# A fused attention and feed-forward kernel: the last quarter of the second weight matrix is issued by another engine's queue

## The chip, the cores and the metric

One core of a Trainium2 chip. The metric is the device time of one execution in microseconds, median of three runs: 299.79 us (299.73 to 300.87). The engines are TensorE (PE, matmuls), VectorE (DVE), ScalarE (ACT), GpSimd (POOL) and SyncE (SP, which here only issues DMA transfers). SyncE and GpSimd each issue DMA transfers into a queue of their own; the transfers of all queues are carried by the core's 16 DMA engines.

## The reference

Windowed attention over 8 batches of 8 heads, 576 positions of 64, window 32 to each side; its output, as 4608 tokens of 512, goes through a feed-forward layer with a tanh GELU.

```python
scores = scale * np.matmul(q, k.transpose(0, 1, 3, 2))
mask = np.abs(pos[:, None] - pos[None, :]) <= 32
scores = np.where(mask, scores, -1e9)
attn = exp(scores - max); attn /= attn.sum(-1) + 1e-9
x = matmul(attn, v).transpose(0, 2, 1, 3).reshape(4608, 512)
h = x @ w_in                                   # (512, 2048)
g = 0.5 * h * (1 + tanh(c * (h + 0.044715 * h**3)))
out = g @ w_out                                # (2048, 512)
```

## The kernel before

The tokens are worked on in nine tiles (`t`) of 512. For each tile there is a first product (`ffn_in`, L545: `ph` or `mm` from `xT` and `w_in16`), a GELU on ScalarE (L553, into `gT`), and a second product with `w_out16`. While tile t's second product runs, the attention of batch t + 1 is worked in between its matmuls, so that tile t + 1 finds its `xT`. Every engine runs its instructions in the order in which the program writes them; nothing is reordered (`manual_schedule`). An instruction that waits holds up all that stands behind it on its engine, and a transfer is issued when its engine comes to it.

The weights arrive as float32 and are cast to float16. `w_out` (2048 x 512) comes in four quarters of 1 MB, `wo[0]` to `wo[3]`, each into a staging tile `wst` of 128 x 4 x 512 from a pool of five buffers (`stage_w`). A quarter has four blocks of 128 rows (`c` = 0 to 3); `load_w_out(i, w, c0, c1)` (L236) issues the transfer of blocks c0 to c1 of quarter i, and `cast_w` (L240 to L242) casts blocks on VectorE, ScalarE or GpSimd. The batch's values `vr` come in four transfers of 256 KB (`vs(0)` to `vs(3)`, L158) and a tail (`vs(4)`, L156); the tails of queries and keys come by `tails()` (L166, L168).

All of these are issued by SyncE. The program writes, after the first weights are cast (L844 and after), the issues in this order: quarter 1, queries and keys, quarter 2's lower half, more queries and keys, `vs(0)`, quarter 2's upper half, `vs(1)`, quarter 3's lower half, `vs(2)`, `vs(3)`, quarter 3's upper half, `vs(4)`, the tails. After them come the loads of batch 2 (L195, L188, L202, L203), whose place in the program is later, but whose buffers are free early.

Tile 0's second product is `ffn_out_0(t4, fc)` (L691): 64 matmuls of 128 x 512, one for each step i = 0 to 63 of the loop at L951, in the order `ORDER_0`: i = 0 to 15 use w_out's blocks 0 to 3 (quarter 0), 16 to 31 blocks 4 to 7, 32 to 47 blocks 8 to 11, and 48 to 63 blocks 12 to 15 (quarter 3), with blocks 12 and 13 first and 14 and 15 from i = 56 on. What is worked in at which step is written in `PLAN_0`, a table from i to actions:

```python
PLAN_0 = {...  16: "m0", 19: "k2", ..., 38: "w5", 39: "m-1", 41: "r3@1", 43: "e1",
          47: "s3@0 v-1@1 d0 w3 e2", 48: "m3 d1", 52: "e3 d2 d3 x-1", 53: "n2@0",
          55: "u3", 57: "p0@0 p2@1 x0 x1", ...}
```

- `k2` (i = 19): casts of queries and keys of head pair 2 on VectorE, and of batch 0's query tails on GpSimd (L334).
- `e0` (35), `e1`, `e2`, `e3`: the cast of one value block on GpSimd (L329). `d0` to `d3`: copies of value halves on VectorE (L222, L224).
- `w2`, `w5` (28, 38): casts of quarter 2's lower and upper half; in `w5` GpSimd casts block 10 and ScalarE block 11.
- `w3` (47): casts of quarter 3's lower half, block 12 on VectorE, 13 on GpSimd. `u3` (55): the upper half, block 14 on GpSimd, 15 on ScalarE; it also places batch 2's loads (`load_qk(2)`).
- `s`, `m`, `n`, `p`, `v`, `x`: scores and exponentials, masks, sums, products with the values, and the products that give `xT`.

Of the kernel before, what the change touches and what calls it, by code (L numbers as in the profile page):

```python
# [78 lines left out]
def kernel(  # L79
# [9 lines left out]
    nc = tc.nc  # L89
# [115 lines left out]
    def load_v(b, cs=range(4)):  # L205
        V = Vs[b % 2]
        for c in cs:
            nc.gpsimd.dma_start(V[:, c, :, :],  # L208
                                v[b, :, 128 * c:128 * c + 128, :].rearrange("h p d -> p h d"))
# [17 lines left out]
    w_out_v = moe_w_out.rearrange("(c p) f -> p c f", p=128)  # L227

    def stage_w():
        return stage.tile([128, 4, 512], FP32, name="wst", tag="stage")  # L230
# [2 lines left out]
        nc.sync.dma_start(w[:, c0:c1, :], w_in_v[:, c0:c1, 512 * i:512 * i + 512])  # L233
        return w

    def load_w_out(i, w, c0=0, c1=4):  # L236
        nc.sync.dma_start(w[:, c0:c1, :], w_out_v[:, 4 * i + c0:4 * i + c1, :])
        return w

    def cast_w(w, dst, on_dve=(0, 1), cs=range(4), on_act=()):  # L240
# [581 lines left out]
    qk, tails, vs = load_early(1)  # L822
    qk(0)
    wo = [load_w_out(0, stage_w())]
    qk(2)

# [21 lines left out]
    cast_w(wi[1], w_in16[:, :, 512:1024], (0, 2))  # L848
    cast_w(wi[2], w_in16[:, :, 1024:1536], (0, 2))
    wo.append(load_w_out(1, stage_w()))  # L850
    qk(4)
    tails_0("q")
    wo.append(load_w_out(2, stage_w(), 0, 2))
    qk(6)
    vs(0)
    load_w_out(2, wo[2], 2, 4)
    vs(1)
    wo.append(load_w_out(3, stage_w(), 0, 2))
    vs(2, 3)
    load_w_out(3, wo[3], 2, 4)  # L860
    vs(4)
    tails()

# [30 lines left out]
    for t in range(NT):  # L894
# [56 lines left out]
        for i in range(113 if t else 65):  # L951
            if t > 1 and i == 4 and b + 1 < B:
                nc.gpsimd.tensor_copy(after, KLs[b % 2][:, 3, 0:1])  # L953
                load_v(b + 1)
            if t == 1 and i == 94:
                for c in range(4):
                    nc.gpsimd.tensor_copy(Vs[1][:, c, :, :], vrs[3][:, c, :, :])
# [116 lines left out]
```

## Time and profile before

| | |
|---|---|
| median of three runs | 299.79 us (299.73 to 300.87) |
| the profiled execution: its time, its span | 298.71 us, 297.0 us |
| mean granted TensorE clock | 0.999 |
| busy: PE, DVE, ACT, POOL | 287.1, 209.2, 196.4, 89.4 us |
| SyncE's queue (q1) | 38.67 MB, 61.6 % of 16 engines' span |
| GpSimd's queue (q0) | 10.83 MB, 23.0 % |
| first GpSimd transfer in the profile | 76.42 us |
| tile 0's second product (L691) | 34 to 56 us |

The span is the time from the first to the last instruction; the time of the execution is a little longer. The profile is of one execution. All times inside it are microseconds from the span's start. "A <- B" means that A's engine sat idle until B ended. In lists of transfers the last number is the time from the issue to the landing.

### The profile page before, as it was taken

How to read it: one execution, taken by the hardware profiler on the slowest of the kernel's cores; microseconds unless marked ns; L12 is line 12 of the kernel's file. 1: busy time of each engine (PE TensorE's matmuls, PEld its weight loads, DVE VectorE, ACT ScalarE, POOL GpSimd, SP SyncE). 2: the span in 40 equal slices, each digit the busy share in tenths (PEclk: the TensorE clock that was granted, in tenths of full speed). 3: DMA queues.
4: the chain of work that ended last, by engine and by line, in shares of the span. 5: the costliest groups of instructions: out<-in, count | busy, mean ns of one | idle time of the engine just before them, and what ended most of it. 6: DMA issues, size and time to landing. Idle time of an engine off the chain costs nothing.

```text
span 297.0 us, 7282 instructions
## 1 busy us (share of the span) xinstructions
PE 287.1 (97%) x2949; PEld 184.7 (62%) x2949; DVE 209.2 (70%) x466; ACT 196.4 (66%) x315; POOL 89.4 (30%) x141
## 2 busy tenths in 40 slices
PE   7889999999999999999999999999999999999993
PEld 3534444446874587458844884488547867786783
DVE  4662475997986676868686879576966776964772
ACT  4876756778587876678657965695669557705800
POOL 3435415201407731406080606060800050015000
PEclk9999999999999999999999999999999999999999
DMA  7999999989999998989997997999594040004013
GB/s 216 263 297 383 366 280 263 264 178 202 291 192 191 235 233 156 145 167 244 150 193 116 253 145 158 142 227 170 102 175 38 0 116 29 2 13 131 0 35 109
DMA packets 116615, 51.01 MB, mean 172 GB/s; under 512 B 98391, under 2 KB 110167, under 8 KB 116582
## 3 DMA queue, kind: packets, MB, share of 16 engines
q1 hardware_dynamic: 91684, 38.67, 61.6%
q0 software_dynamic: 23776, 10.83, 23.0%
q10 hardware_dynamic: 1122, 1.06, 1.1%
q8 instruction: 23, 0.38, 0.6%
q14 instruction: 10, 0.08, 0.1%
HBM read 36.70 MB, written 9.44 MB: 155 GB/s over the span
## 4 chain that ended last, share of the span: by engine, by line
PE 80%; DMA 13%; DVE 2%; SPq 2%; ACT 1%; issue 1%; POOL 0%
PE mm L719 32%; PE mm L545 17%; PE ph L545 15%; DMA wst<-in_moe_w_out_dram 7%; DMA wst<-in_moe_w_in_dram 5%; PE pu L597 3%; PE ps_s L436 3%; PE ps_d L463 2%; DMA tr<-in_k_dram 2%; PE ps_o L473 2%; SPq L254 2%; PE mm L597 1%; PE ps_od L473 1%; PE ps_od L463 1%; PE mm L691 1%; PE py L719 1%
## 5 line engine op out<-in xcount | busy, mean ns | idle before, releaser
L545 PEld LDWEIGHTS <-w_in 128*128 128x128 f16 x512 | 49.7, 98 | 56.9 <-POOL w_in L835 0.5
L545 PE MATMUL ph<-xT,w_in 128*128 128x512 f16 x256 | 64.1, 379 | 0.4 <-POOL w_in L835 0.4
L545 PE MATMUL mm<-xT,w_in 128*128 128x512 f16 x256 | 64.1, 379 | 0.0
L681 POOL DMA_DIRECT2D out_dram<-y x55 | 32.3, 597 | 83.8 <-DVE y L748 75.5
L553 ACT ACTIVATE gT<-mm 128x512 f16<-128x512 f32 x60 | 35.6, 598 | 33.1 <-PE mm L545 32.5
L719 PEld LDWEIGHTS <-s 128*128 128x128 f16 x512 | 49.3, 98 | 7.1 <-DVE s L662 0.6
L719 PE MATMUL mm<-t,s 128*128 128x256 f16 x376 | 45.2, 273 | 0.3 <-DVE y L732 0.2
L662 DVE TENSOR_TENSOR s<-gT 128x512 f16<-128x512 f16 x64 | 27.2, 426 | 19.0 <-ACT gT L553 18.8
L719 PEld LDWEIGHTS <-gT 128*128 128x128 f16 x384 | 36.2, 98 | 6.5
L553 ACT ACTIVATE gT<-ph 128x512 f16<-128x512 f32 x58 | 32.2, 600 | 10.9 <-PE ph L545 10.9
L449 ACT ACTIVATE pe<-ps_s 128x960 f16<-128x960 f32 (+1 forms) x31 | 29.5, 974 | 13.9 <-PE ps_s L436 13.8
L719 PE MATMUL mm<-w_out,gT 128*128 128x256 f16 x256 | 32.6, 273 | 0.0
L104 ACT ACT_TABLE_LOAD x18 | 23.1, 1283 | 2.2 <-issue 1.9
L498 ACT ACTIVATE lt<-ps_d 128x480 f32<-128x480 f32 (+2 forms) x28 | 15.6, 556 | 10.4 <-PE ps_d L463 6.9
L499 ACT ACTIVATE lt<-lt 128x480 f32<-128x480 f32 (+3 forms) x36 | 21.1, 585 | 1.1
L458 DVE TENSOR_TENSOR pe<-pe,band 128x960 f16<-128x960 f16 x28 | 18.6, 683 | 2.3 <-ACT pe L449 2.3
L473 PEld LDWEIGHTS <-V 128*64 128x64 f16 x520 | 13.8, 111 | 6.3 <-DVE V L218 1.2
L719 PE MATMUL mm<-t,gT 128*128 128x256 f16 x128 | 16.1, 273 | 0.0
L208 POOL DMA_DIRECT2D V<-in_v_dram x16 | 14.3, 909 | 1.1 <-POOL after L953 0.4
L662 DVE TENSOR_TENSOR s<-s,gT 128x512 f16<-128x512 f16 x32 | 13.9, 434 | 1.1
L719 PE MATMUL mm<-w_out,s 128*128 128x256 f16 x120 | 14.6, 273 | 0.0
L508 DVE TENSOR_TENSOR xT<-ps_o,lt 128x480 f16<-128x480 f32 (+5 forms) x26 | 13.4, 536 | 1.1 <-PE ps_o L473 1.1
(146 smaller groups left out, 387.1 us busy)
## 6 DMA issues: line engine op xcount, KB each, us to landing
kr<-in_k_dram SPq DMA_DIRECT2D x31, 256.0 KB, 10.0
qr<-in_q_dram SPq DMA_DIRECT2D x6, 1024.0 KB, 6.9
wst<-in_moe_w_in_dram SPq DMA_DIRECT2D x7, 512.0 KB, 8.4
wst<-in_moe_w_out_dram SPq DMA_DIRECT2D x2, 1024.0 KB, 11.6
wst<-in_moe_w_out_dram SPq DMA_DIRECT2D x4, 512.0 KB, 5.8
qr<-in_v_dram SPq DMA_DIRECT2D x8, 256.0 KB, 5.6
V<-in_v_dram POOLq DMA_DIRECT2D x16, 128.0 KB, 8.8
qr<-in_q_dram SPq DMA_DIRECT2D x7, 256.0 KB, 6.9
```

The source lines that it names most:

```text
L104: nc.scalar.add_instruction(mybir.InstLoadActFuncSet(name=nc.get_next_instruction_name(), act_func_set_id=which, ins=[], outs=[]))
L208: nc.gpsimd.dma_start(V[:, c, :, :], v[b, :, 128 * c:128 * c + 128, :].rearrange("h p d -> p h d"))
L449: nc.scalar.activation(pe, ps[:, :, 0:w], AF.Exp, scale=SCALE)
L458: nc.vector.tensor_tensor(pe, pe, m.rearrange("k (o j) p -> k o j p", o=1).broadcast_to(list(pe.shape)), op=ALU.mult)
L473: nc.tensor.matmul(o[64 * h:64 * h + 64, cols].rearrange("d (j p) -> d j p", j=4)[:, :, p0 - q0:p1 - q0], Vs[b % 2][:, slot, 2 * pr + h, : ...
L498: nc.scalar.activation(lt[:, 0:n], d[:, 0:n], AF.Ln)
L499: nc.scalar.activation(lt[:, 0:n], lt[:, 0:n], AF.Exp, scale=-1.0)
L545: nc.tensor.matmul(ph, w_in16[:, dc, fc * 128:fc * 128 + 128], xT[:, dc, t * 512 % RING:t * 512 % RING + 512], start=(dc == 0), stop=(dc = ...
L553: nc.scalar.activation(gTs[t][:, fc, :], phs[fc], AF.Gelu_apprx_tanh)
L662: nc.vector.tensor_tensor(dst, x, y, op=op)
L681: eng.dma_start(out_v[b, j, q0 + p:q0 + p + e, cols], yo[m:m + e, cols])
L719: nc.tensor.matmul(pys["apart"][:, 0:256] if apart else py[:, blk, :], lhsT, wino[w][:, f, :], start=(new and i % (8 if one else 16) == 0) ...
```

## The change

`load_w_out` gets a parameter for the queue. The two issues of quarter 3 are taken out of SyncE's order (`vs(1)`, `vs(2)`, `vs(3)`, `vs(4)` then follow one another), while the staging buffer is taken at the same place. They are written into step i = 20 of tile 0's loop, on GpSimd's queue, both halves one after the other. On GpSimd they stand directly behind the cast of query tails (L334, i = 19) and ahead of the first value cast (L329, i = 35). The casts of the quarter stay where they are (i = 47 and 55), and wait for GpSimd's transfers instead of SyncE's.

```diff
-    def load_w_out(i, w, c0=0, c1=4):
-        nc.sync.dma_start(w[:, c0:c1, :], w_out_v[:, 4 * i + c0:4 * i + c1, :])
+    def load_w_out(i, w, c0=0, c1=4, queue=nc.sync):
+        queue.dma_start(w[:, c0:c1, :], w_out_v[:, 4 * i + c0:4 * i + c1, :])
         return w
...
     vs(1)
-    wo.append(load_w_out(3, stage_w(), 0, 2))
+    wo.append(stage_w())
     vs(2, 3)
-    load_w_out(3, wo[3], 2, 4)
     vs(4)
     tails()
...
                 load_v(b + 1)
+            if t == 0 and i == 20:
+                load_w_out(3, wo[3], 0, 2, nc.gpsimd)
+                load_w_out(3, wo[3], 2, 4, nc.gpsimd)
             if t == 1 and i == 94:
```

## The prediction

> **What bounds the kernel now.** I read the page's busy shares first (PE 287.1 us of a span of 297.0: 97 %), then TensorE's own waits, then the chain of waits in order of time, then SyncE's and GpSimd's timelines around tile 0's second product, last the DMA answers. The chain of waits, in order of time (start, duration, what):
>
> ```profile
> 26.55 11.24 DMA wst<-in_moe_w_out_dram
> 37.81 8.40 DMA wst<-in_moe_w_out_dram
> 46.26 0.62 POOL w_out L242
> 46.92 0.38 PE mm L691
> ...
> 49.04 0.36 PE ps_s L436 x16
> 49.43 0.98 ACT pe L449
> 50.43 0.66 DVE pe L458
> ...
> 53.28 0.30 DVE V L224
> 53.62 0.98 PE ps_od L473 x40
> ```
>
> Until 46.9 us the end is set by a transfer: the upper half of w_out's third quarter, issued at 37.81, lands 8.40 us later, GpSimd casts its first block, TensorE goes on. From there on the chain runs over TensorE's order, an exponential, a mask and copies of values, and after 56 us almost only over TensorE. So whoever delays that landing delays everything; and nothing here can make it earlier, since it is issued before the place of the change. TensorE's waits between 34 and 57 us (us in total, times, longest):
>
> ```profile
> PE mm L691 <- POOL w_out L242: 0.9, 2, 0.5
> PE mm L691 <- DVE w_out L242: 0.6, 1, 0.6
> ```
>
> The 0.6 is at 33.96 us, ahead of the change. The 0.9 is 0.48 us at 46.92 (the landing above) and 0.40 us at 52.85 (a cast of the last quarter's upper half). Only the 0.40 belongs to the transfers that the change moves. SyncE issues (start, duration):
>
> ```profile
> 37.81 2.18 SPq L237 DMA_DIRECT2D wst<-in_moe_w_out_dram  x1
> 40.04 1.06 SPq L158 DMA_DIRECT2D vr<-in_v_dram  x1
> 41.20 2.28 SPq L237 DMA_DIRECT2D wst<-in_moe_w_out_dram  x1
> 43.53 2.64 SPq L158 DMA_DIRECT2D vr<-in_v_dram  x2
> 46.21 2.42 SPq L237 DMA_DIRECT2D wst<-in_moe_w_out_dram  x1
> ```
>
> and GpSimd works:
>
> ```profile
> 40.94 0.60 POOL L334 CAST t<-tr 64x512 f16<-64x512 f32 x1 [2.47 <-DMA tr<-in_q_dram]
> 44.58 0.82 POOL L329 CAST V<-vr 128x512 f16<-128x512 f32 x1 [3.04 <-DMA vr<-in_v_dram]
> 46.26 0.61 POOL L242 CAST w_out<-wst 128x512 f16<-128x512 f32 x1 [0.86 <-DMA wst<-in_moe_w_out_dram]
> 47.38 0.61 POOL L329 CAST V<-vr 128x512 f16<-128x512 f32 x1 [0.51 <-DMA vr<-in_v_dram]
> 48.97 0.63 POOL L242 CAST w_out<-wst 128x512 f16<-128x512 f32 x1 [0.98 <-DMA wst<-in_moe_w_out_dram]
> 49.66 1.90 POOL L329 CAST V<-vr 128x512 f16<-128x512 f32 x2
> 52.05 0.75 POOL L242 CAST w_out<-wst 128x512 f16<-128x512 f32 x1 [0.49 <-DMA wst<-in_moe_w_out_dram]
> ```
>
> GpSimd waits for almost every transfer: first values at 44.6, third quarter at 46.2, second values at 47.4, the moved halves at about 48.9 and 52.0. One queue delivers these in the order of issue, about as fast as they are used. The stretches show DMA busy at 0.95 to 1.24 from 36 to 48 us; the six of one microsecond from 42 to 48 moved 305, 309, 268, 347, 302 and 250 GB/s, a mean of 297.
>
> **The change, part by part.** *Removed from SyncE:* two issues, 2.28 + 2.42 = 4.70 us. Behind them stand the third and fourth values, batch 1's tails, and batch 2's queries and keys; they are issued up to 2.3 and 4.7 us earlier. The values end at GpSimd's casts, which the last of them meets without a wait even now (49.66, two in a row); the later loads feed tile 1, where TensorE shows no wait for a transfer. Worth nothing, then; at best the 0.40 us at 52.85, and not even that by the chain, which passes that moment over the mask and the copies of values, not over the weight cast. A gain is thus bounded by 0.40 us.
>
> *Added to GpSimd:* two issues of 512 KB. In the changed program they stand after the cast of query tails (L334, ends 40.94 + 0.60 = 41.54) and before the first cast of values (44.58). The staging buffer is free (its earlier contents were last read at 30.2), so they wait for nothing. Nearest rows: 611 ns for a store of 128 rows on this queue, 909 ns for a value load of 1,024 pieces; so 1.2 to 1.8 us for two, I take 1.2 (these have 256 pieces each). Both bounds fit in the 3.04 us of waiting before 44.58, so what is queued behind them (the value cast and the weight casts) loses nothing; without that cover it would be 1.2 to 1.8 us on the values. GpSimd's later transfers take other semaphores, which costs nothing, as their waits reach eight transfers back as before.
>
> *Moved:* 1 MB, from a place behind the third quarter and between the values to a second queue that is open beside SyncE's. The first half's issue stays where it was (41.55 against 41.20), the second comes 4 us early. This is the part that can cost. How early does its data flow? The shortest landings on GpSimd's queue are 3.4 us for a 160 KB store and 3.6 us for a 64 KB load at 83.2; so the first bytes count from 41.55 + 3.4 = 44.95. At that time SyncE's queue still owes 46.21 - 44.95 = 1.26 us of the third quarter. If both queues share evenly, these 1.26 us take 2.52: the landing slides by 1.26 us. Bounds: 0, if the older queue loses nothing; and 1,048,576 B / 297 GB/s = 3.53 us, if the whole moved megabyte goes first. That queues do take from each other this kernel shows, with the same sequence (one 1 MB query load, four key loads) twice, at 51 and at 73 us, and with a crowd from 105 us on (size, us to landing):
>
> ```profile
> kr<-in_k_dram SPq DMA_DIRECT2D x4, 256.0 KB, 5.4
> kr<-in_k_dram SPq DMA_DIRECT2D x4, 256.0 KB, 7.2
> out_dram<-yo POOLq DMA_DIRECT2D x2, 256.0 KB, 6.5
> kr<-in_k_dram SPq DMA_DIRECT2D x2, 256.0 KB, 13.0
> ```
>
> Alone 5.4 us; beside two 256 KB stores of GpSimd's (76.4 us) 7.2; beside stores and value loads 13.0. Half a megabyte beside it cost 1.8 us, which lies on the side of an even share. I take 1.26.
>
> The Trainium skill has a rule against this change: "DMA: Bandwidth & Descriptors", section "Queues, rings and completion order", says that each DMA engine goes round the queues that have work, a packet at a time, so a second queue gives no new engines and takes its turns from the first. By that rule the third quarter's landing slides by about the 1.26 us; by the reading that a second queue is free it would slide by 0. The 5.4 against 7.2 us agrees with the rule.
>
> *What is late next.* The values go behind the third quarter on SyncE's queue. Work from 44.95 on: 1.26 us for the third quarter, 3.53 for the moved quarter, three values of 262,144 B / 297 GB/s = 0.88, so 2.65; 7.44 in all, and the last value lands by 52.39. GpSimd casts it in 0.80 (mean 803 ns), then the last quarter's third block in 0.73 (mean 726 ns): 53.92, TensorE 0.05 later at 53.97, against 52.85 now: 1.12 us. That lies inside the 1.26 by which TensorE is late already, so the two don't add; the copies of values on VectorE (52.97 + 1.26 = 54.23) find the last cast done at 53.19. The moved halves themselves, at half of 297 GB/s, land at 44.95 + 3.53 = 48.5 and 52.0, against 48.9 and 52.0 now: in time for a TensorE that runs 1.26 us late.
>
> **Sum.** -0 (SyncE's slots) + 0 (GpSimd's issues, hidden) + 1.26 (third quarter) + 0 (values, inside it) = +1.26 us. Nothing downstream takes it back: TensorE is busy nearly without a gap after 56 us. The profiled execution took 298.71 us (span 297.0); with the sum 299.97. The median of the runs is 1.08 us above that execution, so 299.79 + 1.26 = 301.05, which I give as 301.1: 0.42 % slower. A measurement of this kernel can tell from no change what lies over 0.5 %, 1.5 us, so this is just inside "no change".
>
> **Rivals.**
>
> *The queues don't collide in time.* GpSimd's transfers take longer to start than 3.4 us, or the older queue keeps its pace. For it: in the crowd from 97 us on, stores of 112 to 144 KB on GpSimd's queue needed 9.1 to 9.7 us, so the newcomer can be the one that loses. Then the third quarter lands at 46.21 as now, and at best the 0.40 us at 52.85 goes: 299.4 to 299.8. Against it: DMA is full in that stretch, and 5.4 became 7.2. This rival is not slower.
>
> *The moved quarter goes first, or is itself late.* Slower, by one mechanism: GpSimd's queue gets more than its half while the third quarter is under way, so that the cast at 46.26 and the matmul behind it wait for up to the whole megabyte: 3.53 us, 303.3. It decides from a landing 1.5 us late on. For it: 2 KB rows against the 256 B rows of the values, and a DMA that was full before. Against it: the same 9.1 to 9.7 us stores. In the middle between even and whole, (1.26 + 3.53) / 2 = 2.4 us: 302.2.
>
> *It does not do what it says.* If the cast at L334 waited longer for its tails (now it ends 2.47 us of waiting at 40.94), the two issues would go out later. For it: they stand behind that wait on GpSimd. Against it: the tails are issued at 30.12, ahead of all that moves. At 43.5 instead of 41.55 the first bytes count from 46.9, after the third quarter: the first half, alone, would land 1.77 us (524,288 B / 297 GB/s) later, at 48.7, so 299.8.
>
> **How the numbers follow.** Even sharing 0.46 (0.6 to 2.0 us late: 300.4 to 301.8, a little more than half of it below the bound of 301.3); no collision 0.20, with the late issue 0.24; the moved quarter first 0.25; a gain beyond all that I see 0.05. Faster by over 0.5 % needs 1.5 us, where I find 0.40: 0.05. Within 0.5 %: 0.24 and 0.26 of the sharing case, 0.50. Slower by over 0.5 %: 0.25 and the other 0.20 of sharing, 0.45. The range takes in the no-collision case with a few tenths of scatter and the whole megabyte: 299.2 to 303.2; the likeliest case's own range is 300.4 to 301.8.
>
> **What would show it.** In the changed profile: GpSimd's two issues directly after 41.5, 0.6 to 0.9 us each; the weight cast now at 46.26 at about 47.5, and the matmul at 46.92 at about 48.2; the score matmuls of 49.04 at about 50.3; no wait of TensorE for the last quarter beyond 0.4 us; SyncE's values and batch 2's queries issued 2 to 5 us earlier. If the cast still comes at 46.3, the sharing is wrong; if it comes after 48, GpSimd's queue took more than half. If TensorE waits for the casts of the moved quarter (L242 at i = 48 or 56) by more than now, the new queue is the slow one, and my sum has the wrong term.

## The result and the profile after

The changed kernel takes 300.48 us (median of 21 runs, 298.86 to 303.12); the kernel before, in as many runs, 299.35 us (298.38 to 300.95). The ratio is 1.0031, 95 % interval 1.0017 to 1.0046: slower by 0.93 us (0.5 to 1.4); the medians alone lie 1.13 us apart. The profiled execution of the changed kernel has a span of 298.9 us, against 297.0.

The chain of waits of the changed kernel, in order of time (start, us, what):

```profile
25.80 11.11 DMA wst<-in_moe_w_out_dram
...
36.92 2.12 SPq L237
...
42.86 9.04 DMA vr<-in_v_dram
...
51.96 0.64 POOL V L329
52.59 0.57 POOL w_out L242
...
53.21 0.38 PE mm L691
```

Before, this stretch hung on the landing of the third quarter (its upper half, blocks 10 and 11) at 46.2. Now it hangs on the last value: landed 9.04 us after its issue, cast by GpSimd, and only then GpSimd's next instruction, the cast of w_out's block 14, for which TensorE waits. TensorE's own waits over the whole run:

```profile
PE mm L691 <- POOL w_out L242: 2.0, 2, 1.1
PE ps_s L436 <- DMA KT<-k: 1.5, 1, 1.5
```

The first were 0.9 us before. They are the waits at i = 40 and i = 56; first the kernel before, then the changed one:

```profile
46.92 0.38 PE L691 MATMUL mm<-w_out,gT 128*128 128x512 f16 x1 [0.48 <-POOL w_out L242]
52.85 0.38 PE L691 MATMUL mm<-w_out,gT 128*128 128x512 f16 x1 [0.40 <-POOL w_out L242]
```

```profile
46.40 0.38 PE L691 MATMUL mm<-w_out,gT 128*128 128x512 f16 x1 [0.81 <-POOL w_out L242]
53.21 0.38 PE L691 MATMUL mm<-w_out,gT 128*128 128x512 f16 x1 [1.14 <-POOL w_out L242]
```

The wait for transposed keys (`KT`) is at 225 us and is treated below: it comes and goes in both kernels. SyncE and then GpSimd of the changed kernel in order of time (start, us, what, and in brackets the idle time before):

```profile
36.92 2.12 SPq L237 DMA_DIRECT2D wst<-in_moe_w_out_dram  x1
39.09 6.37 SPq L158 DMA_DIRECT2D vr<-in_v_dram  x3
45.50 3.54 SPq L156 DMA_DIRECT2D vt<-in_v_dram  x1
49.15 0.72 SPq L166 DMA_DIRECT2D tr<-in_q_dram  x1
```

```profile
40.92 1.65 POOL L237 DMA_DIRECT2D wst<-in_moe_w_out_dram  x2
43.93 0.61 POOL L329 CAST V<-vr 128x512 f16<-128x512 f32 x1 [1.35 <-DMA vr<-in_v_dram]
45.73 0.61 POOL L242 CAST w_out<-wst 128x512 f16<-128x512 f32 x1 [1.19 <-DMA wst<-in_moe_w_out_dram]
46.87 0.61 POOL L329 CAST V<-vr 128x512 f16<-128x512 f32 x1 [0.52 <-DMA vr<-in_v_dram]
48.27 0.61 POOL L242 CAST w_out<-wst 128x512 f16<-128x512 f32 x1 [0.79 <-DMA wst<-in_moe_w_out_dram]
50.68 0.68 POOL L329 CAST V<-vr 128x512 f16<-128x512 f32 x1 [1.79 <-DMA vr<-in_v_dram]
51.96 0.64 POOL L329 CAST V<-vr 128x512 f16<-128x512 f32 x1 [0.60 <-DMA vr<-in_v_dram]
52.54 0.61 POOL L242 CAST w_out<-wst 128x512 f16<-128x512 f32 x1
```

This execution ran 0.8 us ahead of the other one until 34 us, so times are to be compared from the second product's start: its first matmul is at 33.17, against 33.96. SyncE got rid of two issues (4.70 us), yet the query tails go out at 49.15, against 49.38, no earlier by that start: the three values now take 6.37 us to issue (1.06 + 2.64 before) and the value tail 3.54 (0.61). What was freed went into the next issues, which took longer. On GpSimd the last cast, of block 14, no longer waits for its own transfer: it starts at 52.54, when the cast ahead of it ends. The moved transfers' landings (size, us from issue), the two halves:

```profile
wst<-in_moe_w_out_dram POOLq DMA_DIRECT2D x1, 512.0 KB, 7.3
wst<-in_moe_w_out_dram POOLq DMA_DIRECT2D x1, 512.0 KB, 8.0
```

So the upper half, issued at about 41.8, was there at about 49.8, 2.7 us before GpSimd came to its cast; the value that is cast ahead of it came at 51.9.

VectorE waits for the same value. Its last copies of values, which the products with the values need:

```profile
52.63 0.67 DVE L222 COPY V<-V 64x512 f16<-64x512 f16 x1 [0.51 <-POOL V L329]
53.31 0.28 DVE L224 COPY V<-V 64x512 f16<-64x512 f16 x1
```

They end at 53.59, 2.50 us before tile 1's first matmul (56.09). In the kernel before, where these products wait for the last copy, it ends 2.49 us before that matmul (53.57, 56.06). So in the changed kernel the late value reaches TensorE by two paths that end together: over block 14's cast, which the chain names, and over the copies.

As a yardstick I take the length of tile 0's second product, from the start of its first matmul (L691) to that of tile 1's first (L545), in each profile. Times and ratios are of many runs, the lengths of one execution each.

| kernel | second product, us | ratio to before (95 %) |
|---|---|---|
| before; again | 22.10; 22.16 | 1 |
| the change; again; a third time | 22.92; 24.47; 22.35 | 1.0031 (1.0017 to 1.0046) |
| e1, upper half on GpSimd | 23.01 | 1.0057 (1.0034 to 1.0080) |
| e2, lower half on GpSimd | 21.90 | 1.0013 (0.9997 to 1.0029) |
| e3, both halves early, on SyncE | 22.76 | 1.0022 (0.9999 to 1.0044) |
| e4, both on GpSimd, at i = 35 | 24.55 | 1.0057 (1.0034 to 1.0080) |
| e5, lower at i = 20, upper at i = 38 | 22.72 | 0.9999 (0.9984 to 1.0015) |
| e6, the change, block 14 cast first | 22.53 | 1.0009 (0.9992 to 1.0027) |
| e7, no transfer of the quarter | 22.08 | one execution only |
| c1, before, third quarter ahead of values | 22.05 | 1.0016 (0.9996 to 1.0037) |
| c2, the change, likewise | 22.35 | 1.0025 (1.0001 to 1.0049) |

### The profile page after: what moved, and what is told of

It is laid out like the page before. It is cut to its first block, busy times and chain, and to the rows that moved or that the text cites. A ratio compares the mean times of both kernels' runs of the same rounds, so it can differ in the third digit from the quotient of the medians.

```text
span 298.9 us, 7280 instructions
## 1 busy us (share of the span) xinstructions
PE 286.3 (96%) x2949; PEld 184.0 (62%) x2949; DVE 210.6 (70%) x466; ACT 196.4 (66%) x315; POOL 89.7 (30%) x143
## 3 DMA queue, kind: packets, MB, share of 16 engines
q10 hardware_dynamic: 1122, 1.06, 1.1%
## 4 chain that ended last, share of the span: by engine, by line
PE 76%; DMA 16%; SPq 4%; DVE 1%; ACT 1%; issue 0%; POOL 0%
PE mm L719 32%; PE mm L545 16%; PE ph L545 14%; DMA wst<-in_moe_w_in_dram 5%; DMA wst<-in_moe_w_out_dram 4%; PE pu L597 3%; DMA vr<-in_v_dram 3%; PE ps_s L436 3%; DMA KT<-k 3%; PE ps_d L463 2%; PE ps_o L473 2%; DMA tr<-in_k_dram 2%; SPq L254 2%; SPq L158 1%; PE mm L597 1%; PE ps_od L473 1%
## 5 line engine op out<-in xcount | busy, mean ns | idle before, releaser
L545 PEld LDWEIGHTS <-w_in 128*128 128x128 f16 x512 | 49.6, 98 | 56.9 <-issue 0.5
L545 PE MATMUL ph<-xT,w_in 128*128 128x512 f16 x256 | 64.1, 379 | 0.4 <-POOL w_in L835 0.4
L545 PE MATMUL mm<-xT,w_in 128*128 128x512 f16 x256 | 64.1, 379 | 0.0
L436 PE MATMUL ps_s<-QT,KT 64*64 64x128 f16 (+3 forms) x576 | 13.5, 216 | 1.8 <-DMA KT<-k 1.5
L436 PEld LDWEIGHTS <-KT 64*64 64x64 f16 x576 | 10.0, 106 | 7.7 <-issue 3.8
```

Source lines behind the costliest of these rows:

```text
L436: nc.tensor.matmul(sides[h][64 * half:64 * half + 64, 4 * n * r:4 * n * r + 4 * n].rearrange("k (j p) -> k j p", j=4)[:, :, p0 - q0:p1 - q ...
L545: nc.tensor.matmul(ph, w_in16[:, dc, fc * 128:fc * 128 + 128], xT[:, dc, t * 512 % RING:t * 512 % RING + 512], start=(dc == 0), stop=(dc = ...
```

## The experiments

The theory, formed on the profile above: the upper half is needed last but arrives early, at the cost of values that are needed before it. The rivals: the second queue costs as such; the third quarter's landing is all of the cost; the cost lies in later tiles.

**Half of the change at a time: e1 and e2.**

```diff
-    wo.append(stage_w())
+    wo.append(load_w_out(3, stage_w(), 0, 2))      # e1: lower half on SyncE
...
-                load_w_out(3, wo[3], 0, 2, nc.gpsimd)
                 load_w_out(3, wo[3], 2, 4, nc.gpsimd)
```

> Only the upper half of the last quarter goes by GpSimd's queue at i = 20; the lower half stays on SyncE between the second and third values. Theory (the values, 256 B rows behind a shared DMA, come late, and GpSimd's cast of block 14 stands behind the last value's cast): half the megabyte beside the values, so the last value lands about half as late as with the whole (1.4 us late there, so about 0.7), TensorE's wait at i = 56 is 0.4 to 0.8 us, the third quarter is late by at most 0.4 us; +0.3 to +0.7 us on the kernel before. Rival (the cost is the second queue as such, from its first transfer on): as much as the whole change, +0.9 us. Rival (the cost lies in later tiles): no change of the waits in tile 0, +0.9 us all the same.

```diff
     vs(2, 3)
+    load_w_out(3, wo[3], 2, 4)                     # e2: upper half on SyncE
...
                 load_w_out(3, wo[3], 0, 2, nc.gpsimd)
-                load_w_out(3, wo[3], 2, 4, nc.gpsimd)
```

> Only the lower half goes by GpSimd's queue at i = 20; the upper half stays on SyncE behind the fourth value. Theory: the lower half competes with the third quarter as in the change (third quarter 0.3 to 0.4 us late), but SyncE's values come hardly later than before, as the same bytes stood before them; the wait at i = 56 is on the upper half's landing, 0.4 to 0.7 us; +0.3 to +0.5 us. Rival (the second queue as such): +0.9 us. Rival (later tiles): waits of tile 0 as before, +0.9 us.

Measured: e1 1.0057, e2 1.0013. The upper half alone costs 1.7 us, no less than the whole change and far over the 0.3 to 0.7 expected (its one profile shows 0.9 us of it); the lower alone costs 0.4 us with an interval that reaches to nothing. TensorE and GpSimd of e1:

```profile
51.05 0.84 PE L691 MATMUL mm<-w_out,gT 128*128 128x512 f16 x2 [0.59 <-DVE w_out L242]
```

```profile
50.60 0.87 POOL L242 CAST w_out<-wst 128x512 f16<-128x512 f32 x1 [2.25 <-DMA wst<-in_moe_w_out_dram]
51.42 1.65 POOL L329 CAST V<-vr 128x512 f16<-128x512 f32 x2
```

Here I had the wrong victim: not the values but the lower half of the same quarter, left on SyncE, is what the upper half overtakes. It lands 8.87 us after its issue at 41.67 by e1's chain of waits (7.7 in the kernel before, by GpSimd's cast at 48.97), and blocks 12 and 13, due at i = 48, are late. By the same chain VectorE's mask and copies, which stand behind its cast of block 12, end the stretch. The values behind that half are cast without a wait. In e2 the order of landing is that of need, and the second product is as short as before (21.90 us; the wait that I expected at i = 56 is not there). GpSimd's queue as such is not the cost.

**The order without the second queue: e3.**

```diff
-    wo.append(stage_w())
+    wo.append(load_w_out(3, stage_w(), 0, 2))
+    load_w_out(3, wo[3], 2, 4)
     vs(2, 3)
...
-                load_w_out(3, wo[3], 0, 2, nc.gpsimd)
-                load_w_out(3, wo[3], 2, 4, nc.gpsimd)
```

> Both halves stay on SyncE, but together, between the second and the third values: the order of the change without a second queue. Theory: the third quarter lands as before (wait at i = 40 about 0.5 us), the third and fourth values come one half-quarter later, the last at about 51.5 to 52.5, so GpSimd's cast of block 14 stands behind it and TensorE waits 0.7 to 1.1 us at i = 56; +0.4 to +0.7 us. Rival (the second queue as such costs, the order does not): as before, within 0.2 us. Rival (third quarter's landing is the whole cost): within 0.2 us.

Measured 1.0022 (0.66 us), 22.76 us. GpSimd of e3:

```profile
52.02 0.62 POOL L329 CAST V<-vr 128x512 f16<-128x512 f32 x1 [1.54 <-DMA vr<-in_v_dram]
52.89 0.68 POOL L329 CAST V<-vr 128x512 f16<-128x512 f32 x1 [0.24 <-DMA vr<-in_v_dram]
53.51 0.68 POOL L242 CAST w_out<-wst 128x512 f16<-128x512 f32 x1
```

With one queue GpSimd waits for a value, then for the last, and block 14 goes behind, as in the changed kernel. TensorE waits 0.58 us for it, less than the 0.7 to 1.1 expected. But this wait does not end the stretch. The chain of waits of e3 runs, as in the kernel before, over the third quarter's landing, the mask and the copies:

```profile
54.66 0.30 DVE V L224
55.00 0.98 PE ps_od L473 x42
```

The cost has the expected size, but the interval just reaches 1, and this profile does not show that the late values caused it. That the order alone costs as much on one queue is likely and not shown.

**Both halves later: e4.**

```diff
+                    if t == 0 and g == 0:               # behind the cast e0
+                        load_w_out(3, wo[3], 0, 2, nc.gpsimd)
+                        load_w_out(3, wo[3], 2, 4, nc.gpsimd)
```

> Both halves by GpSimd's queue, but issued behind the first value's cast (i = 35, about 44.6 us) instead of at i = 20. Theory: the third quarter lands as before, the wait at i = 40 is 0.5 us; the quarter's data flow from about 47.5, its lower half lands at 50 to 51.5, so that TensorE waits for the casts at i = 48 by 1 to 2 us; the values are late as in the change; +1.0 to +2.5 us. Rival (the third quarter's delay is the whole cost): as before or faster, -0.4 to +0.3 us.

Measured 1.0057, 24.55 us: inside the expected cost, partly for a reason that I had not expected. GpSimd and TensorE of e4:

```profile
46.49 1.64 POOL L237 DMA_DIRECT2D wst<-in_moe_w_out_dram  x2
48.14 0.62 POOL L242 CAST w_out<-wst 128x512 f16<-128x512 f32 x1
```

```profile
48.81 0.38 PE L691 MATMUL mm<-w_out,gT 128*128 128x512 f16 x1 [1.66 <-POOL w_out L242]
```

The two issues take 1.64 us of GpSimd and stand right before the cast of block 10, which follows without a wait: GpSimd's issue time, hidden at i = 20, is in the way here. TensorE's wait at i = 40 is 1.66 us, against 0.48 before; without the issues GpSimd might have waited here for the third quarter, so the price is at most the 1.64. Another 0.69 us are waited for at i = 48 and 0.54 at i = 56.

**Only the upper half later: e5.**

```diff
                 load_w_out(3, wo[3], 0, 2, nc.gpsimd)      # i = 20
-                load_w_out(3, wo[3], 2, 4, nc.gpsimd)
...
+                        if g == 5:                          # behind w5, i = 38
+                            load_w_out(3, wo[3], 2, 4, nc.gpsimd)
```

> Both halves by GpSimd's queue, the lower at i = 20 as in the change, the upper behind the cast of block 10 (i = 38, about 47 us), when the third quarter has landed. Theory (the cost is the upper half going ahead of transfers that are needed earlier, whichever queue it is on): the second product of tile 0 takes about as long as in the kernel before (22.1 us from its first matmul to the first of tile 1), as with the lower half alone moved (21.9); the upper half lands at 51.5 to 53, the wait at i = 56 is 0.2 to 0.8 us; -0.2 to +0.6 us on the kernel before. Rival (GpSimd's queue as such costs, for each half): as the change, 22.9 us, +0.8 to +1.0 us.

Measured 0.9999: the loss is gone though both halves use GpSimd's queue. The one profile shows 22.72 us, with waits of 0.67, 0.28 and 0.63 us; that lies above the length that I expected, so the time, not this profile, carries the verdict. It does not beat the kernel before. It also speaks against the third quarter's landing as the cost: this profile waits 0.67 us at i = 40, longer than the 0.48 of the kernel before, in a kernel that takes no longer.

**Is it the values or the cast that stands behind them? e6.**

```diff
-                        cast_w(wo[g], w_out16[:, 12:16, :], cs=(0, 1), on_dve=(0,))
+                        cast_w(wo[g], w_out16[:, 12:16, :], cs=(0, 1, 2), on_dve=(0,))
...
-                    cast_w(wo[g], w_out16[:, 12:16, :], on_act=(3,), cs=(2, 3))
+                    cast_w(wo[g], w_out16[:, 12:16, :], on_act=(3,), cs=(3,))
```

> The change, with GpSimd's cast of block 14 at i = 47, ahead of the third and fourth values' casts, instead of at i = 55. Theory A (the late last value is the cost, by the copies of values on VectorE and the products behind them): TensorE's wait at i = 56 goes, but the products with the values wait in its place; the second product takes 22.5 to 22.9 us, against 22.9 in the change; 0 to -0.4 us on the change. Theory B (only the block's cast is late, because it stands behind the last value's cast): the second product takes 22.0 to 22.3 us, -0.6 to -0.9 us on the change.

Measured 1.0009, that is 0.22 % or 0.66 us below the change's ratio, with intervals that overlap. TensorE and VectorE of e6:

```profile
54.38 0.98 PE L473 MATMUL ps_od<-pe,V 128*64 128x64 f16 x46 [0.37 <-DVE V L224]
```

```profile
52.82 0.58 DVE L222 COPY V<-V 64x512 f16<-64x512 f16 x1
53.42 0.29 DVE L224 COPY V<-V 64x512 f16<-64x512 f16 x1
53.74 0.29 DVE L222 COPY V<-V 64x512 f16<-64x512 f16 x1
54.04 0.28 DVE L224 COPY V<-V 64x512 f16<-64x512 f16 x1
```

The wait at i = 56 is gone. What ends the stretch now is the chain that ended it in the kernel before, scores, mask, copies, products, and these copies show no wait for a value. The time lies in the range of theory B (only block 14's cast is late), the length of 22.53 us at the lower end of that of theory A (the copies are late). In the changed kernel both paths end together (above), and here the last copy ends 2.50 us before tile 1's first matmul again (54.32, 56.82). So moving the cast takes one of the two paths away, and which of them alone would have cost how much stays open.

**The quarter left out: e7.**

```diff
-    wo.append(stage_w())
+    stage_w()
+    wo.append(wo[2])
...
-                load_w_out(3, wo[3], 0, 2, nc.gpsimd)
-                load_w_out(3, wo[3], 2, 4, nc.gpsimd)
```

> The last quarter is not transferred at all; its casts read the third quarter's staging tile in its place. Shows what the values need alone. By the forecast's rate of 297 GB/s (0.88 us for a value) the last of the three values behind the third quarter lands 2.7 us behind it; if rows of 256 B alone go at the 165 to 193 GB/s that the changed kernel shows from 49 to 52 us, a value takes 1.4 to 1.6 us and the last lands 4.1 to 4.8 us behind the third quarter. The third quarter lands 7.8 to 8.4 us after its issue as in the kernel before; no wait at i = 48 and 56; the second product takes 21.3 to 21.8 us.

GpSimd of e7:

```profile
46.57 0.61 POOL L242 CAST w_out<-wst 128x512 f16<-128x512 f32 x1 [0.61 <-DMA wst<-in_moe_w_out_dram]
...
49.69 0.65 POOL L329 CAST V<-vr 128x512 f16<-128x512 f32 x1 [0.66 <-DMA vr<-in_v_dram]
```

The last value is cast 3.1 us behind the third quarter's block, 1.04 us for a value: 262,144 B / 1.04 us = 252 GB/s, nearer to the forecast's 297 than to the slow rate that I had come to suspect. And 22.08 us is no shorter than before: with no transfer of the quarter at all the copies and the products still end the stretch. The expected 21.3 to 21.8 us missed this. The one execution took 302.09 us, 2.6 of it in waits for transposed keys in later tiles.

**The third quarter ahead of the values: c1 (from before) and c2 (from the change).**

```diff
-    vs(0)
     load_w_out(2, wo[2], 2, 4)
-    vs(1)
+    vs(0, 1)
...
-PLAN_0 = {... 35: "e0", ..., 38: "w5", ...}
+PLAN_0 = {... 38: "w5 e0", ...}
```

> The kernel before, with the third quarter's upper half issued ahead of the first value instead of behind it, and the first value's cast behind that of block 10 (i = 38) instead of at i = 35. Theory (the landing of that half is a wait on the path only by its 0.48 us at i = 40; behind it the chain of scores, mask, copies and products ends the stretch): the half is issued up to 2 us earlier and lands 1 to 2 us earlier, the wait at i = 40 goes, and the second product takes 21.5 to 22.0 us; 0 to -0.5 us. Rival (the values are as urgent as the weights): the values' casts come later, the copies wait, 0 to +0.5 us.

> The same exchange in the changed kernel. If the changed kernel loses by the third quarter's landing, most of the loss goes: no wait at i = 40, second product 22.0 to 22.5 us, 0 to +0.4 us on the kernel before. If it loses by the values (theory), these stand even later, behind the moved quarter: TensorE waits 1 to 2 us at i = 56 or for the copies, second product 22.7 to 24 us, +0.6 to +2 us.

Measured 1.0016 and 1.0025. TensorE of c2:

```profile
53.60 0.38 PE L691 MATMUL mm<-w_out,gT 128*128 128x512 f16 x1 [1.34 <-POOL w_out L242]
```

In both the wait at i = 40 is gone, as expected, and in both TensorE waits at i = 56 instead (1.40 us in c1, 1.34 in c2). In c2 the chain runs over the last value's landing, 7.10 us after its issue, and the two casts. In c1 GpSimd's cast of block 14 waits 1.53 us for the upper half's own landing. So curing the third quarter's landing does not clearly cure the changed kernel: a longer wait later takes its place. By its time (0.75 us, 0.0 to 1.5) and its wait c2 lies where the values were said to be the cost, by its length of 22.35 us where the third quarter was; alone it does not decide, and e5 speaks more clearly. c1 gains nothing either, so the 0.48 us that the kernel before waits at i = 40 are not worth having.

**The two kernels again.**

> The kernel before once more, for a second profile of it. The second product takes 22.0 to 22.4 us again, with TensorE's two waits at 0.4 to 0.5 us each. Differences elsewhere are the scatter between executions.

> The change once more, for a second profile. Theory (all of the cost lies in tile 0's second product): that takes 22.7 to 23.1 us again, with TensorE's two waits for GpSimd's casts at 0.7 to 0.9 and 1.0 to 1.3 us, and the 1.5 us that TensorE waited for transposed keys at 225 us are not there. Rival (GpSimd's shifted transfers make the later transposes late each time): the wait at 225 us is there again, 1 to 2 us.

> The change a third time: its two profiles had 22.9 and 24.5 us for the second product, the third quarter landing 8.8 and 9.6 us after its issue (8.4 in the kernel before). If the shares of the two queues differ from execution to execution, the third quarter's landing is again between 8.4 and 9.8 us and the second product between 22.5 and 24.5 us; the wait for transposed keys at 225 us, there in one of the two, need not be.

TensorE of the change's second profile, then of its third:

```profile
48.47 0.38 PE L691 MATMUL mm<-w_out,gT 128*128 128x512 f16 x1 [1.75 <-POOL w_out L242]
53.18 0.38 PE L691 MATMUL mm<-w_out,gT 128*128 128x512 f16 x1 [1.37 <-POOL w_out L242]
```

```profile
47.63 0.38 PE L691 MATMUL mm<-w_out,gT 128*128 128x512 f16 x1 [0.31 <-POOL w_out L242]
54.17 0.38 PE L691 MATMUL mm<-w_out,gT 128*128 128x512 f16 x1 [0.85 <-POOL w_out L242]
```

The cost in tile 0 comes again each time but not in one size: 0.2 to 2.4 us over the 22.1 of before; the third quarter lands (GpSimd's cast of block 10, less the issue) 8.8, 9.6 and 8.1 us after its issue (8.5 and 7.9 in the two profiles of before) and the values behind it shift as well. The third profile lies below both ranges expected of it. In the second the chain runs over another value: the second one landed 11.25 us after its issue, and block 13's cast stood behind its cast, though the lower half was there at 49.8 (8.0 us from issue); TensorE's 1.37 us at 53.18 are this wait, at i = 48. On average the second product is 23.25 us, 1.1 over the 22.13 of before, which accounts for the 0.93. The kernel before hangs less on these waits than I expected: its second profile shows no wait of TensorE for GpSimd's casts, and yet 22.16 us. The wait for transposed keys is 1.5, none and 0.7 us in the three profiles of the change, and none and 0.7 us in the two of before: scatter, which settles the rival of the later tiles in its stated form. From tile 1's first matmul to the end of the span the change took 242.8, 241.0 and 241.8 us, before 240.9 and 241.7; a few tenths there could not be told from scatter.

## Why the prediction held, point by point

*What bounds it.* Right: both profiles of the kernel before hang on the third quarter's landing, and from there on scores, mask, copies and products.

*SyncE's slots are worth nothing, the gain at most 0.40 us.* Right, and more than that: in e7's profile not even the absence of the transfer shortens the stretch. Of "issued up to 2.3 and 4.7 us earlier" the first came true: by the second product's start the third value went out 2.3 us earlier (7.30 us behind it, against 9.57). The second did not: the issues lengthened, and from the query tails on nothing went out notably earlier.

*GpSimd's issues.* Right: 1.65 us, inside the bounds of 1.2 to 1.8, with 1.35 us of waiting left before the first value's cast. e4 shows the two issues without the cover, 1.64 us right in front of a cast.

*The third quarter, 1.26 us by even shares.* The direction was right, the size too large: in the profiled execution its landing took 8.8 us, so measured, instead of 8.5, and TensorE's wait at i = 40 grew from 0.48 to 0.81. Against the two profiles of before, the three of the change average 8.8 against 8.2 us, so 0.7, with ranges that overlap. The changed profile's transfers from GpSimd's first data to the third quarter's landing show why (packets, MB, share of the 16 engines; q0 is GpSimd's queue, q1 SyncE's):

```profile
DMA packets 749, 0.57 MB, mean 321 GB/s; under 512 B 628, under 2 KB 628, under 8 KB 749
q0 software_dynamic: 86, 0.34, 59.2%
q1 hardware_dynamic: 663, 0.24, 54.9%
```

This is 43.9 to 45.68 us. The 628 small packets are the values' (256 B each); beside GpSimd's 86 that leaves 35 of SyncE's with rows of the weights, by my estimate 0.07 MB or 0.24 us at 297 GB/s. The sum had counted all that SyncE's queue moves until the landing as the third quarter's, 1.26 us; most of it was values already.

*The values, 1.12 us and inside the 1.26.* This is the term that was put at nothing and was not. The sum had the last value 4.9 us behind the third quarter (52.39 against 47.47); it was 6.2 us (51.90 against 45.68). GpSimd's second casts wait for it, and TensorE's wait at i = 56 grew from 0.40 to 1.14 us, on top of the 0.33 at i = 40. The mechanism had been named, GpSimd's casts in order with block 14 last, but the even share failed here: the third value took from 46.9 to 50.7, 3.8 us, while in e7 all three took 3.1. The two queues from 45 to 47 us, behind the third quarter:

```profile
q0 software_dynamic: 170, 0.63, 88.1%
q1 hardware_dynamic: 252, 0.06, 16.1%
```

Against the values' pieces of 256 B GpSimd's queue moved ten times the bytes of SyncE's (in the other two profiles of the change 0.30 against 0.04 and 0.34 against 0.03 MB from 46 to 47). So the moved halves were there at 48.2 and 49.8, where the sum had 48.5 and 52.0, and the values paid. A row for weights beside values was needed, and half-and-half was taken.

*The sum.* In the profiled pair: first matmul to i = 40 later by 0.27 us, from there to i = 56 by 0.88, then 0.33 given back, because the products with the values no longer wait for the copies while they run (1.12 us instead of 1.45): 0.82 us. The forecast had 1.26 + 0; by the runs it is 0.93 us (0.5 to 1.4). The total came near because one term was too large and the other, taken for hidden, was not: that part is luck. (The range ends at 303.2, though its text takes in the whole megabyte, priced at 303.3.)

*Its signs.* The issues came as named. The cast of block 10 was named for about 47.5, and one at 46.3 as a sign against the sharing: counted from the second product's start it came 0.26 us later than before (12.56 against 12.30), which speaks against the 1.26. And TensorE waited longer at i = 56, the sign for a wrong term in the sum; the new queue was not the slow one, though, its halves came early.

*The rivals.* "No collision" falls with the late values; the third quarter's landings alone (8.1 to 9.6 us against 7.9 and 8.5) would not exclude it. "The moved quarter goes first" is partly what happens, not to the third quarter as I had it, but to the values; one execution in three (24.47 us) did come close to its middle price of 2.4 us. "It does not do what it says": the issues went out at 40.92, directly behind the cast, as forecast.

*The Trainium skill.* The rule of "DMA: Bandwidth & Descriptors", section "Queues, rings and completion order", that an engine goes round the queues with work packet by packet, was the reason against an open second queue. The changed kernel agrees with it in kind: a value that needs about 1.04 us alone needed 3.8 us beside the moved quarter. No run here shows what a packet is for the one queue and for the other.

## What to carry to other kernels

Moving a transfer to a second queue made no room here; it changed the order in which a full set of DMA engines served the transfers. Before moving one, write down when each transfer in flight is needed, and keep the one that is needed last from starting early (e5 against the change: the same queue for both halves, 0.9999 against 1.0031). Look at the size of the pieces too: the transfers in 256 B pieces were the ones that gave way. An engine that casts in order turns one late landing into the lateness of everything that it casts after it, even of data that landed 2.7 us before (block 14).

## What was not expected

SyncE's freed time came to nothing because its issues stretch: the value tail, issued in 0.61 us before, took 3.54 us in the changed kernel, 3.36 in e3 and 4.00 in c2. Toward the end of such an issue and behind it the DMA was not always full while values were awaited. One stretch of the changed kernel and one of e3 (from and to, length, busy time and count of TensorE, its weight loads, VectorE, ScalarE and GpSimd, then the clock, the DMA share and GB/s):

```profile
50.00:51.00 1.00, 1.00 (x8) 0.31 (x6) 0.95 (x3) 0.56 (x2) 0.32 (x1) 1.00 0.85 169
```

```profile
51.00:52.00 1.00, 1.00 (x6) 0.38 (x4) 0.57 (x2) 0.97 (x3) 0.00 (x0) 1.00 0.31 70
```

A share of 0.31 in the midst of the 1.54 us that GpSimd waits for a value (e3, until 52.02) means that bandwidth alone is not the explanation of the late values; what holds an issue of SyncE for 3.5 us, and why the engines then run dry, was not tried and stays open. VectorE's copies of value halves took 0.29 us or about 0.6 us (e6: 0.58 and 0.29 within one microsecond), the longer ones mostly beside a cast of GpSimd's; that too was only seen, not tested.
